# A spectral block and a feed-forward block in one kernel: the first stage in written orders, the first chunk handed over already transposed

## The chip, the cores and the metric

The kernel runs on one core of one Trainium2 chip. Times are device microseconds (us). The measure is the median of separate runs; a profile is one further execution, and it gives a time of its own and a span (first to last instruction).

The engines are called as the profile calls them: PE (TensorE, matmuls), DVE (VectorE), ACT (ScalarE), POOL (GpSimd) and SP (SyncE, which here only issues DMAs, in order).

## The reference

```python
def _layernorm(x, axis=-1, eps=1e-5):
    m = jnp.mean(x, axis=axis, keepdims=True)
    v = jnp.var(x, axis=axis, keepdims=True)
    return (x - m) / jnp.sqrt(v + eps)

# x [1, 2048, 512] bf16, A_w_r and A_w_i [2048, 257], w1 [512, 1792], w2 [1792, 512]
X = rfft2(layernorm(x)) * (A_w_r + 1j * A_w_i)     # over both axes, float32
h = x + irfft2(X, s=(2048, 512)).astype(bf16)
u = einsum("bsd,df->bsf", layernorm(h), w1) + b1
r = maximum(u, 0)
out = h + einsum("bsf,fd->bsd", r * r, w2) + b2
```

## The kernel before

The 2048 rows are held as 16 tiles of 128 rows (`xs[:, g, :]`, g from 0 to 15). The two-dimensional transform is done as chains of matmuls against sine and cosine tables that the kernel makes itself.

**Front.** POOL and DVE make integer index tables, ACT turns them into sines: `KF` (the 128-point mask table, made on DVE at L342 from `kft`), `GF`, `EF` (parts 0 and 1 by sine, part 2 the negative of part 0). DVE takes the row statistics of 14 of the 16 tiles (`st`, L393, then `mv`, L395), ACT those of tiles 3 and 6 (L384, L387). POOL raises the variance to the power -1/2 (`rs`, L400), and each tile's scaled table `KR` is `KF` times `rs`: tiles 0 to 7 on POOL, 8 and 9 on ACT, 10 to 15 on DVE. PE multiplies each tile by its `KR` (L416, L417), and ACT and DVE copy the result into `Bt` (L432 on ACT for tiles 0 to 9, L448 for 10 to 15).

**Middle.** For eight pairs of blocks `pr` = 0 to 7 there follow: matmuls `p2` (L516; the first one needs all of `Bt`), the copy `U` (L526), matmuls `p3` (L495, with `EF`), the copy `AB` (L593; L554 for pair 0), on DVE the sum and difference `X` (L600), the product with the spectral weights `m` (L614), `Z` (L624) and `M` (L635, L637), matmuls `p4` (L654 to L662, with the transposed tables `EI`), and the copy into `T2` (L677). `EI` parts 0 and 1 come from SP's DMA transposes of `EF` (L453), part 2 is made by ACT from part 0 (L482). `EN` (L485, in the order lists `EI-3-6`) is a negated slice of `EI`, used by pair 6 alone. The inverse table `GI` is made by ACT in the middle (L260). Weights arrive in two halves: the natural rows (`Wn`, L283 and L284) and the reversed rows, which are first copied inside DRAM (`wx`, L279) and then loaded (`Wr`, L287). Pair 0 needs only `Wn`; every other pair needs both.

**Hand-over.** For tiles 0 and 1 (chunk 0): matmuls `pd` (L738), copies `EO` (L743), matmuls `py` that add the residual and give h in natural layout (L828 to L833), the statistics of h (tile 0 on ACT, L689; tile 1 on DVE, L843 and L845), a square root (L846), reciprocal (L849), normalization `u` (L857, L859), PE transposes (L868), the copy `UT` (L874), and then the first matmuls of the feed-forward part.

**Feed-forward.** Chunks of 2, 3, 4, 4 and 3 tiles: for each, 14 up-projections (L936), ReLU with bias on ACT (L948), the square on DVE (L954), the down-projections (L965), the residual (L974) and the store. The spectral tail of the later chunks (L765 to L820) is put between the up-projections.

**What sets the order.** `Plan` holds tasks with an engine, a guessed duration, the keys that they read and write and a priority. It picks for each engine the task that can start first by its own guesses; `lag` is how long after its issue a DMA is guessed to land, and `order` only fixes a sequence in the plan. `plan.run(MID)` takes the middle's order of PE, ACT and DVE from lists of names written by hand. The program's order on each engine is then fixed (`pin`); on the chip an instruction waits for what it really depends on. In PSUM, `mm` tiles have three slots in the middle and `sg` tiles two.

```python
dve(1.14, prod, z, reads=[("X", pr), ("Wn", 0), ("Wn", 1), ("Wr", 0), ("Wr", 1)],
    writes=[("m", pr)], alloc=("m", ("m", pr)))
act(0.37, lambda pr=pr: sc.activation(EN[:, BY_Z.index(pr)], EI[:, 0:2, pr], ACT.Identity, scale=-1.0), 84.0,
    reads=[("EI", 0), ("EI", 1)], writes=[("EI", 3, pr)])
"ACT": "U-2 AB-1 U-3 AB-2 U-5 AB-3 EI-2 b1f U-4 AB-5 U-6 AB-4 T2-0 T2-1 U-7 GI EI-3-6 AB-6 T2-2 "
       "AB-7 T2-3 T2-5 sqrt T2-4 T2-6 T2a-0 T2b-0",
```

Of the kernel before, what the change touches and what calls it, by code (L numbers as in the profile page):

```python
# [15 lines left out]
P = 128  # L16
# [17 lines left out]
class Plan:  # L34
# [55 lines left out]
    def run(self, line=None):  # L90
# [8 lines left out]
        while any(left.values()):  # L99
            best = None  # L100
            for e, ts in left.items():
                cand = []
                for t in ts if e not in lines else [t for t in ts if t["name"] == lines[e][0]] if lines[e] else []:
# [29 lines left out]
            if e in lines:  # L133
                lines[e].pop(0)
# [10 lines left out]
def kernel(  # L145
# [47 lines left out]
    mv2 = persist.tile([P, 2], FP32, name="mv2")  # L193
    st2 = persist.tile([P, 6], FP32, name="st2")
# [22 lines left out]
    cE = tab.tile([P, 1], FP32, name="cE")  # L217
    rowq = tab.tile([P, 2, 16], I32, name="rowq")
# [50 lines left out]
    CH = ((0, 2), (2, 4), (4, 6), (6, 8), (8, 12), (12, 16))  # L269
    LAND = (2.65, 3.85, 4.55, 5.2, 5.95, 6.7)  # L270
# [3 lines left out]
    add("SP", 0.2, lambda: sy.dma_start(b1b[:], B_b1.rearrange("(i p) -> i p", p=P)), writes=["b1b"], prio=5.5, at=0.7, lag=8.0)  # L274
# [3 lines left out]
    for i in range(2):  # L278
        add("SP", 2.0, lambda i=i: sy.dma_start(wx[i][:].rearrange("k j l -> j k l"),  # L279
                                                wv[i].rearrange("k j l -> j k l")[9:16, ::-1, 1:L + 1]),  # L280
            writes=[("wx", i)], prio=6 + i, at=1.0, lag=5.0)
    for i in range(2):
        add("SP", 1.0, lambda i=i: (sy.dma_start(W[:, i], wv[i][:, 0:8, 1:L + 1]),  # L283
                                        sy.dma_start(W[:, 2 + i, 0], wv[i][:, 8, 1:L + 1])), writes=[("Wn", i)],  # L284
            prio=8 + i, at=1.0, lag=12.0)
    for i in range(2):
        add("SP", 1.0, lambda i=i: sy.dma_start(W[:, 2 + i, 1:8], wx[i][:, ::-1]), reads=[("wx", i)], writes=[("Wr", i)],  # L287
            prio=10 + i, lag=10.5)
# [29 lines left out]
    pool(0.1, lambda: gp.memset(ident[:], 0.0), 390.0, writes=["id0"], order=[("KR", G - 1)])  # L318
    pool(0.3, lambda: gp.affine_select(out=ident[:], in_=ident[:], compare_op=ALU.not_equal, fill=1.0, base=0,
                                       pattern=[[-1, P]], channel_multiplier=1), 390.0, reads=["id0"], writes=["ident"])  # L320
    pool(0.34, lambda: iota(idxD[:], [[1, 256]], 0, 0), 395.0, writes=["idxD"], order=[("KR", G - 1)])
# [15 lines left out]
    for t in range(2):  # L337
# [4 lines left out]
    dve(0.48, lambda: ve.scalar_tensor_tensor(  # L342
        KF[:].rearrange("p h (q s) -> p (h q) s", s=8), sub8[:].unsqueeze(1).to_broadcast([P, 32, 8]), pF[:, 2:3],
        flat(kft[:]).unsqueeze(2).to_broadcast([P, 32, 8]), ALU.is_equal, ALU.mult),
        0.7, reads=["kft", "pF", "sub8"], writes=["KF"], shared=True)
# [7 lines left out]
    for t in range(2):  # L353
        act(0.62, lambda t=t: sin_of(flat(GF[:, t]), lo(flat(fiG[:, t]))), 0.6 + t / 10, reads=[("fiG", t)],
            writes=[("gf", t)])
    dve(0.15, lambda: ve.tensor_scalar(GF[:, :, :, 255:256], GF[:, :, :, 255:256], 0.5, None, ALU.mult), 54.0, reads=[("gf", 0), ("gf", 1)],
        order=[("KR", G - 1)], writes=["GF"])
    for i in range(2):
        act(1.16, lambda i=i: sin_of(flat(EF[:, i]), lo(fiE[i][:])), 0.5 + i / 10, reads=[f"fiE{i}"],
            writes=[f"EF{i}"])  # L360
    dve(0.46, lambda: ve.tensor_scalar(EF[:, 2], EF[:, 0], -1.0, None, ALU.mult), 78.0, reads=["EF0"],
        order=["BtD"], writes=["EF2"])
# [17 lines left out]
    for bi, (a, b) in enumerate(BATCH):  # L380
# [38 lines left out]
    for g in range(BIG):  # L419
# [10 lines left out]
        def e1(g=g, key=key):  # L430
            dst = Bt[:].rearrange("p e q (g s) -> p e g q s", s=8)[:, :, g - 1:g + 1]
            sc.copy(dst, T[key][:].rearrange("p (i e q s) -> p e i q s", e=4, q=16, s=8))  # L432
        if g % 2:
            act(0.93, e1, 10 + g, reads=[key], writes=["Bt"] + ["Btw"] * (g == BIG - 1))
    for a, b in UNITS:
        n = b - a
        for t in range(2):
            k, eng = ("p1", a, t), ("ACT", "DVE")[t]
# [7 lines left out]
            def e2(a=a, b=b, t=t, k=k, eng=eng):  # L446
                dst = Bt[:, 2 * t:2 * t + 2].rearrange("p e q (g s) -> p e g q s", s=8)[:, :, a:b]
                COPY[eng](dst, T[k][:, 0:256 * (b - a)].rearrange("p (i e q s) -> p e i q s", e=2, q=16, s=8))  # L448
            add(eng, ((0.37, 0.59), (0.42, 0.67))[t][n - 1], e2, reads=[k] + ["Btw"] * t, order=[("va", 4)] * t,
                writes=["Bt"] + ["BtD"] * (t == 1 and b == G), prio=56 + a)  # L450

    def tr_dma(i, dst, src, dep, prio):
        add("SP", 2.5, lambda: sy.dma_start(dst, src, transpose=True), reads=dep, writes=[("EI", i)], prio=prio, lag=(10.6, 10.4, 0, 8.0)[i])  # L453
    for i in range(2):
        tr_dma(i, EI[:, i], flat(EF[:, i]), [f"EF{i}"], 12 + i)
    tr_dma(3, KI[:], flat(KF[:]), ["KF"], 16)
    for k, (d, s) in ((0, (W1[:], B_w1.rearrange("(c p) f -> p c f", p=P))),
# [7 lines left out]
    dve(0.25, lambda: ve.tensor_scalar(CN[:, 0:len(BY_PE)], EF[:, 1, PE0:8], -1.0, None, ALU.mult), 75.0, reads=["EF1"],  # L465
        order=["EF2"], writes=["CN"])
    dve(0.13, lambda: ve.tensor_copy(pF[:, 5:7], pI[:, 5:7]), 0.75, reads=["p2"], writes=["pF2"], shared=True)
    for lt in range(4):
        pool(0.48, lambda lt=lt: gp.tensor_scalar(fiI[:, lt], idxD[:], pF[:, 5 + lt % 2:6 + lt % 2],
                                                  float((QT, HT)[lt // 2]), ALU.mult, ALU.add), 400.0,  # L470
             reads=["pF2", "idxD", ("KR", G - 1)], writes=["fiI"])
    dve(0.15, lambda: ve.tensor_scalar(nm1[:], mv1[:, :, 0], -1.0, None, ALU.mult), 190.0,
        reads=[("mv", g) for g in range(G)], order=["EF2"], writes=["nm0"])
    dve(0.15, lambda: ve.tensor_scalar(nm1[:, 3:7:3], nmr[:, 3:7:3], 1.0 / RT, None, ALU.mult), 190.0,
        reads=["nm0"], writes=["nm1"], shared=True)

    def mid_tasks():
        def b1t():
            mm(sg_tile(("b1",))[:, 0:NF], lhsT=b1b[:], rhs=ident[0:NF, 0:NF], start=True, stop=True)
        add("PE", 0.07, b1t, reads=["b1b", "ident"], order=[("p3", 3)], writes=[("b1",)], prio=141.0, alloc=("sg", ("b1",)))  # L480
        act(0.19, lambda: sc.copy(b1f[:], T[("b1",)][:, 0:NF]), 142.0, reads=[("b1",)], writes=["b1f"])
        act(1.1, lambda: sc.activation(flat(EI[:, 2]), flat(EI[:, 0]), ACT.Identity, scale=-1.0), 83.0, reads=[("EI", 0)],  # L482
            order=["EF2", ("X", 0, 0)], writes=[("EI", 2)])
# [3 lines left out]
        act(1.07, lambda: sin_of(flat(GI[:]), lo(flat(fiI[:]))), 142.0, reads=["fiI"], order=[("p3", 4)], writes=["GI"])  # L487
        act(1.4, lambda: sc.activation(junk[:, 0:1], eps[:], ACT.Sqrt), 0.0, reads=["GI", "eps", ("p4", SQ)], writes=["sqrt"])
# [8 lines left out]
    for pr, first in ((0, 1), (1, 1), *((p, 0) for p in range(8))):  # L497
        z = Z0 + 10 * pr
        if (pr, first) == (0, 0):
            plan.run()  # L500
# [121 lines left out]
        def zz(pr=pr, r=0):  # L622
            Z = buf(fwd, ("Z", pr), "Z", [P, 2, 2, 256], BF16, 2) if r == 0 else T["Z", pr]
            ve.tensor_tensor(Z[:, :, r], T["m", pr][:, :, 0, r], T["m", pr][:, :, 1, 1 - r], (ALU.subtract, ALU.add)[r])  # L624
# [18 lines left out]
        def s4(pr, part, lts):  # L643
            key = ("p4", pr, "t", lts[0] // 2) if pr == 7 else ("p4", pr)
            pt = T[key] if part else (sg_tile if pr == 7 else mm_tile)(key)
            src = T["M" if pr and pr not in BY_Z else "Z", pr][:].rearrange("p u r (j e) -> p u r e j", e=2)
            for lt in lts:
                r, e = lt // 2, lt % 2
                k = lt - lts[0] if pr == 7 else lt
# [11 lines left out]
                else:  # L661
                    mm(o, lhsT=src[:, part, r, e, :], rhs=EI[:, 1 - part:3 - part, pr, :],  # L662
                       start=part == 0 and e == 0, stop=part == 1 and e == 1)
        for h in range(2):
            for k in range(2) if pr == 7 else (None,):
                lts = {None: range(4) if pr else (2 * h, 2 * h + 1), 0: (0, 1), 1: (2, 3)}[k]
                add("PE", 0.92 if pr in BY_Z else 0.46 if k is None else 0.23, lambda pr=pr, h=h, s4=s4, lts=lts: s4(pr, h, lts),
                    reads=[("Z", pr) if pr == 0 else ("ZM"[pr not in BY_Z] + "h" * (1 - h), pr), ("EI", 0), ("EI", 1), ("EI", 2)]
                    + [("EI", 3, pr)] * (pr in BY_Z), order=[("p4", pr, 0, k)] * h, uses=[("ZM"[pr > 0 and pr not in BY_Z], pr)],
                    writes=[("p4", pr, h, k)] + [("p4", pr)] * (k is None) + [("p4", pr, "t", k)] * (k is not None),  # L670
                    name=f"p4-{pr}-{h}" + "ab"[k] * 1 if k is not None else f"p4-{pr}-{h}", prio=z + 32 * (pr < 5),
                    alloc=(("mm", ("p4", pr)) if k is None else ("sg", ("p4", pr, "t", k))) if h == 0 else None)

        def et(eng=sc.copy, pr=pr, a=0, b=G, l0=0, l1=4):
            dst = T2[:, l0:l1, a:b, 2 * pr:2 * pr + 2, :].rearrange("p l g q s -> p l q g s")
            src = T["p4", 7, "t", l0 // 2] if pr == 7 else T["p4", pr]
            eng(dst, src[:].rearrange("p (l q g s) -> p l q g s", q=2, g=G, s=8)[:, :, :, a:b])  # L677
# [332 lines left out]
```

## Time and profile before

| | |
|---|---|
| median of 3 runs | 160.2 us (159.95 to 160.39) |
| time of the profiled execution | 160.21 us |
| its span | 158.4 us, 2890 instructions |
| granted clock of PE | 1.0 throughout |
| PE busy | 152.0 us (96% of the span) |
| DVE, ACT, POOL busy | 119.0, 102.5, 33.1 us |

The span splits into stages at these points of the trace: to 18.6 us the front, to 45.3 us the middle, to 51.7 us the hand-over of chunk 0, to 155.5 us the feed-forward part, where PE is busy 103.7 of 103.8 us, and a last output and store. PE also runs matmuls on a zero tile (L243, L368, L716) where the plan sees a gap, so its busy share before 51.7 us says little; which instruction waits for which is what counts there.

### The profile page before, as it was taken

To read this page: it belongs to the slowest core of one execution; us is meant where nothing else is said; L and a number is where in the kernel's file an instruction comes from. 1 tells how busy PE (TensorE), PEld (TensorE's weight loads), DVE (VectorE), ACT (ScalarE), POOL (GpSimd) and SP (SyncE) were. 2 spreads that over 40 slices of the span, in tenths; PEclk is the share of its full clock that TensorE was granted. 3 is DMA by queue.
4 is the path that set the end of the run, shared out by engine and by line. 5 is a ranking of instruction groups with operands and counts; after the bars stand their busy time and mean duration, and the time that the engine had idled before them with its cause. 6 is when DMAs were issued, how large, how long until landed. Compare 5 with 4: busy or idle time off the path is not lost.

```text
span 158.4 us, 2890 instructions
## 1 busy us (share of the span) xinstructions
PE 152.0 (96%) x1027; PEld 91.9 (58%) x1027; DVE 119.0 (75%) x322; ACT 102.5 (65%) x189; POOL 33.1 (21%) x83
## 2 busy tenths in 40 slices
PE   6998999999798999999999999999999999999992
PEld 4587876787477886565544544444544444565471
DVE  5999988999867987889952989991599962285221
ACT  8989679999967887297801899530588820188000
POOL 8798700000000033022240013440002240000000
DMA  4957999994000001104132000314000312010011
GB/s 128 320 187 219 242 226 218 387 363 140 0 4 0 0 4 35 35 33 35 35 66 67 33 0 4 66 35 132 33 0 0 69 36 66 33 35 4 0 66 33
DMA packets 21017, 13.43 MB, mean 85 GB/s; under 512 B 9738, under 2 KB 19722, under 8 KB 21002
## 3 DMA queue, kind: packets, MB, share of 16 engines
q1 hardware_dynamic: 21002, 13.25, 31.3%
q8 instruction: 8, 0.13, 0.3%
q14 instruction: 7, 0.06, 0.1%
HBM read 8.92 MB, written 3.01 MB: 75 GB/s over the span
## 4 chain that ended last, share of the span: by engine, by line
PE 74%; DVE 15%; DMA 4%; issue 3%; SPq 1%; ACT 1%; POOL 0%; ACTq 0%
PE po L965 31%; PE sg L936 20%; PE ph L936 10%; DMA xs<-in_A_x_dram 4%; DVE Z L624 3%; DVE m L614 3%; DVE st L393 3%; DVE X L600 2%; PE m_p L516 2%; PE pp L788 1%; DVE M L635 1%; PE pp L795 1%; SPq L272 1%; DVE M L637 1%; PE s_p L516 1%
## 5 line engine op out<-in xcount | busy, mean ns | idle before, releaser
L965 PE MATMUL po<-W,act 128*128 128x512 bf16 (+1 forms) x238 | 50.0, 366 | 0.0
L948 ACT ACTIVATE rl<-sg,b1f 128x384 bf16<-128x384 f32 (+2 forms) x46 | 27.3, 601 | 21.9 <-PE sg L936 20.6
L936 PEld LDWEIGHTS <-W 128*128 128x128 bf16 x288 | 26.8, 98 | 19.7 <-issue 0.2
L936 PE MATMUL sg<-UT,W 128*128 128x384 bf16 (+2 forms) x184 | 37.2, 337 | 0.0
L965 PEld LDWEIGHTS <-act 128*128 128x128 bf16 x238 | 23.2, 98 | 24.0
L954 DVE TENSOR_TENSOR act<-rl 128x384 bf16<-128x384 bf16 (+2 forms) x70 | 25.0, 367 | 6.5 <-ACT rl L948 6.0
L974 DVE TENSOR_TENSOR ot<-po,hb 128x512 bf16<-128x512 f32 (+1 forms) x17 | 11.2, 658 | 20.7 <-PE po L965 20.5
L880 POOL TENSOR_SCALAR rs<-ss 128x1 f32<-128x1 f32 x14 | 6.1, 435 | 90.5 <-ACT junk L689 90.5
L948 ACT ACTIVATE rl<-ph,b1f 128x512 bf16<-128x512 f32 (+2 forms) x23 | 13.8, 602 | 10.0 <-PE ph L936 9.4
L936 PE MATMUL ph<-UT,W 128*128 128x512 bf16 (+3 forms) x96 | 19.9, 330 | 0.1
L816 DVE TENSOR_TENSOR hs<-pp,xs 128x512 bf16<-128x512 f32 x14 | 9.6, 689 | 2.3 <-PE pp L788 1.3
L689 ACT ACTIVATE junk<-hs,nm 128x512 bf16<-128x512 bf16 x14 | 10.0, 714 | 0.1
L495 PE MATMUL m_p<-U,EF 128*128 128x512 bf16 (+1 forms) x46 | 9.5, 337 | 0.0
L393 DVE BATCH_NORM_STATS2 st<-xs 128x6 f32<-128x512 bf16 x14 | 9.0, 672 | 0.6 <-DMA xs<-in_A_x_dram 0.6
L811 DVE TENSOR_TENSOR R<-q 128x127 bf16<-128x127 f32 x40 | 9.4, 283 | 0.0
L820 DVE TENSOR_TENSOR hb<-hs,b2b 128x512 f32<-128x512 bf16 x14 | 9.1, 681 | 0.0
L882 POOL TENSOR_TENSOR rs<-rs,mhalf 128x1 f32<-128x1 f32 x14 | 8.0, 569 | 1.2
L778 DVE TENSOR_TENSOR q<-pp,od 128x256 f32<-128x256 f32 x20 | 7.6, 415 | 0.0
L243 PEld LDWEIGHTS <-fz 128*128 128x128 bf16 x59 | 5.0, 113 | 4.2 <-issue 2.3
L516 PE MATMUL m_p<-GF,Bt 128*128 128x256 bf16 x56 | 7.4, 273 | 0.0
L677 ACT CAST T<-m_p 128x1024 bf16<-128x1024 f32 x7 | 7.1, 1057 | 0.5 <-PE m_p L659 0.5
L593 ACT CAST AB<-m_p 128x1024 bf16<-128x1024 f32 x7 | 7.3, 1046 | 0.0
(163 smaller groups left out, 227.6 us busy)
## 6 DMA issues: line engine op xcount, KB each, us to landing
W<-in_B_w_dram SPq DMA_DIRECT2D x2, 1792.0 KB, 10.7
out_dram<-ot SPq DMA_DIRECT2D x15, 128.0 KB, 1.8
xs<-in_A_x_dram SPq DMA_DIRECT2D x4, 256.0 KB, 3.8
xs<-in_A_x_dram SPq DMA_DIRECT2D x2, 512.0 KB, 6.7
W<-wx SPq DMA_DIRECT2D x2, 448.0 KB
W<-in_A_w_r_dram SPq DMA_DIRECT2D x1, 512.0 KB, 8.0
W<-in_A_w_i_dram SPq DMA_DIRECT2D x1, 512.0 KB, 6.4
wx<-in_A_w_r_dram SPq DMA_DIRECT2D x1, 448.0 KB
```

The source lines that it names most:

```text
L393: ve.bn_stats(st[:], xs[:, g, :])
L495: mm(o.rearrange("p (j i e) -> p j i e", e=2, i=RUN), lhsT=w, rhs=U[:, q, s].rearrange("p (j e i) -> p j i e", e=2, i=RUN), **k)
L516: mm(puv[:, e, :], lhsT=Bt[:, 2 * t + 1 - e, 2 * pr + q, :], rhs=gfv[:, t, :, e, :], start=(t == 0), stop=(t == 1))
L689: sc.activation(junk[:], src, ACT.Square, bias=nm1[:, g:g + 1], accum_out=ss2[:, g:g + 1])
L811: ve.tensor_tensor(o, x, y, (ALU.add, ALU.subtract, ALU.subtract, ALU.add)[k])
L816: dve(0.66, lambda g=g: ve.tensor_tensor(hs[:, g, :], T["p6", g][:], xs[:, g, :], ALU.add), z, reads=[("p6", g)], writes=[("hs", g)])
L820: add(("DVE", "POOL")[HBP], (0.62, 1.3)[HBP], lambda g=g: (ve, gp)[HBP].tensor_tensor(hb[:, g, :], hs[:, g, :], b2b[:], ALU.add), prio=lat ...
L936: mm(p[:, P * i0:P * i1], lhsT=W1[:, d, bass.ts(f, P)], rhs=T["UT", c][:, i0:i1, d, :], start=(d == 0), stop=(d == ND - 1))
L948: sc.activation(r[:, 0:P * n], T["ph", c, f][:, 0:P * n], ACT.Relu, bias=b1f[:, f:f + 1], scale=1.0)
L954: ve.tensor_tensor(t[:, f, 0:P * n], r[:, 0:P * n], r[:, 0:P * n], ALU.mult)
L965: mm(p[:, cs], lhsT=T["act", c][:, f, bass.ts(i, P)], rhs=W2[:, f, cs], start=(f == 0), stop=(f == NF - 1))
L974: ve.tensor_tensor(o[:, cs], T["po", g, h][:, cs], hb[:, g, cs], ALU.add)
```

## The change

It touches the front, the middle and the hand-over; the feed-forward part stays but for the PSUM tag of one early up-projection and some order keys.

- The front gets written orders for all five engines, SP included (`FRONT`), the middle gets new ones (`MID`), and the hand-over gets some (`DRAIN`).
- `KF` is made by POOL with a two-input multiply. `KR`, the `Bt` copies, `GF`'s correction, `EF` part 2, `CN` and `nm1` may now sit on other engines; by the lists DVE makes `KR` of tiles 5, 7, 10, 13 and 15, ACT of 12, POOL the rest; DVE copies `Bt-9` and `Bt-12-1`, ACT all other `Bt`; POOL makes `EF` part 2.
- `GI` moves into the front on ACT, in two halves. `EI` part 2 becomes a third DMA transpose.
- The fifth load of x (4 tiles) becomes two of 2. SP's order becomes x, `b1b`, `Wn`, `wx`, `EI-0`, `Wr`, `EI-1`, `EI-2`, `EI-3` (`KI`), feed-forward weights.
- In the middle, `p3-1` goes ahead of `p2-2`, `EI-3-6` to the third place on ACT, and `Z` of pair 6 gets a layout in which its two halves don't interleave.
- Chunk 0 is made transposed: `yt` collects mean correction (`cen`), residual (`res`) and spectral part with the feature dimension on the partitions; ACT squares it, PE sums over partitions with a matrix of ones, ACT takes the root, DVE the reciprocal, and one DVE multiply gives `UT`. The natural-layout `py` stays, for the residual of the output.

```diff
-    CH = ((0, 2), (2, 4), (4, 6), (6, 8), (8, 12), (12, 16))
+    CH = ((0, 2), (2, 4), (4, 6), (6, 8), (8, 10), (10, 12), (12, 16))
...
-            prio=8 + i, at=1.0, lag=12.0)
+            prio=6.4 + i / 20, at=1.0, lag=9.0)
...
-        add("SP", 1.0, lambda i=i: sy.dma_start(W[:, 2 + i, 1:8], wx[i][:, ::-1]), reads=[("wx", i)], writes=[("Wr", i)],
-            prio=10 + i, lag=10.5)
+        add("SP", 1.0, lambda i=i: sy.dma_start(W[:, 2 + i, 1:8], wx[i][:, ::-1]), reads=[("wx", i)], order=[("EI", 0)], writes=[("Wr", i)],
+            prio=10 + i, lag=8.0)
...
-    dve(0.48, lambda: ve.scalar_tensor_tensor(
-        KF[:].rearrange("p h (q s) -> p (h q) s", s=8), sub8[:].unsqueeze(1).to_broadcast([P, 32, 8]), pF[:, 2:3],
-        flat(kft[:]).unsqueeze(2).to_broadcast([P, 32, 8]), ALU.is_equal, ALU.mult),
-        0.7, reads=["kft", "pF", "sub8"], writes=["KF"], shared=True)
+    pool(0.5, lambda: gp.tensor_tensor(
+        KF[:].rearrange("p h (q s) -> p (h q) s", s=8), sel[:].unsqueeze(1).to_broadcast([P, 32, 8]),
+        flat(kft[:]).unsqueeze(2).to_broadcast([P, 32, 8]), ALU.mult), 0.95, reads=["kft", "sel"], writes=["KF"])
...
+    tr_dma(2, EI[:, 2], flat(EF[:, 2]), ["EF2"], 15)
...
-        act(1.1, lambda: sc.activation(flat(EI[:, 2]), flat(EI[:, 0]), ACT.Identity, scale=-1.0), 83.0, reads=[("EI", 0)],
-            order=["EF2", ("X", 0, 0)], writes=[("EI", 2)])
...
+            FRONT = {
+                "PE": "fa-0 fa-1 fa-2 fa-4 fa-6 fa-5 fa-3 p1a-0 p1-0 p1a-1 p1-1 p1a-2 p1-2 p1a-3 p1-3 p1a-4 "
+                     "p1a-10-1 p1-10-1 p1a-10-0 p1-10-0 p1a-12-0 p1-4 p1-15-0 p1-15-1 p1a-12-1 p1-12-0 p1-12-1 "
+                     "p1-14-0 p1-14-1 p2-1-0 p2-0-0 p2-0-1 p2-1-1 p3-0-0 p3-0-1",
+                "ACT": "sinset kft gf-0 fiE0 sm-3 GI mv-3 GI0 sm-6 EF0 mv-6 gf-1 Bt-1 Bt-3 Bt-5 Bt-7 KR-12 "
+                      "Bt-10-1 Bt-10-0 Bt-15-0 Bt-15-1 Bt-12-0 Bt-14-0 Bt-14-1 EF1 U-0-0 AB-0-0 AB-0-1",
+                "DVE": "eps fz mv1z p02 p01 pF pF2 fiG-0 fiK sel fiG-0+1 cE st-0 st-1 st-2 mv-0 mv-1 mv-2 va-0 "
+                      "st-4 st-5 mv-4 st-7 mv-5 mv-7 va-1 st-8 st-9 mv-8 mv-9 KR-5 st-11 va-2 mv-11 st-10 st-12 "
+                      "mv-10 mv-12 KR-7 va-3 st-15 st-14 mv-15 KR-10 va-5 st-13 mv-14 mv-13 va-4 nm0 qtc GF "
+                      "KR-15 KR-13 Bt-9 Bt-12-1 U-1-0 U-0-1 U-1-1",
+                "POOL": "p0 p7 p1 sub8 idxG p2 offq0 rowq0 idxD offq rowq idxE fiI+1 fiI+3 mhalf fiG-1 fiI+2 "
+                       "fiG-1+1 fiI KF rs-0 KR-1 KR-0 rs-1 KR-2 KR-3 KR-4 rs-2 KR-6 KR-8 rs-3 KR-11 KR-9 rs-5 "
+                       "rs-4 KFq KR-14 nm1 fiE1 id0 EF2 ident CN",
+                "SP": "x-1 x-3 x-5 x-7 x-9 x-11 x-15 b1b Wn-0 Wn-1 wx-0 wx-1 EI-0 Wr-0 Wr-1 EI-1 EI-2 EI-3 FW-0 "
+                     "FW-1 FW-3",
...
     MID = {
...
+        "PE": "p3-1 p2-2-0 p2-2-1 p2-3-0 p2-3-1 p2-5-0 p3-2 p2-5-1 p3-3 b1 p2-4-0 p2-4-1 p3-5 p3-4 "
+             "p2-6-0 p2-6-1 p4-0-0 p4-0-1 p2-7-0 p2-7-1 p4-2-0 p4-2-1 p3-6 p4-1-0 p4-1-1 p3-7 p4-3-0 "
+             "p4-3-1 p4-5-0 p4-5-1 p4-6-0 p4-6-1 yt-1-0 yt-1-1 p4-4-0 p4-4-1 yt-0-0 p4-7-0a p4-7-0b "
+             "p4-7-1a p4-7-1b yt-0-1 pd-0-1 pd-0-0 pd-1-1 pd-1-0",
+        "ACT": "AB-1 U-2 EI-3-6 U-3 AB-2 U-5 AB-3 b1f U-4 nmt AB-5 AB-4 U-6 T2-0 U-7 T2-2 sqrt AB-6 T2-1 "
+              "AB-7 T2-3 T2-5 T2-6 T2-4 T2a-1 EO-0-0 EO-1-0",
...
-            ve.tensor_tensor(Z[:, :, r], T["m", pr][:, :, 0, r], T["m", pr][:, :, 1, 1 - r], (ALU.subtract, ALU.add)[r])
+            ve.tensor_tensor(Z[:, r] if pr in BY_Z else Z[:, :, r], T["m", pr][:, :, 0, r], T["m", pr][:, :, 1, 1 - r],
+                             (ALU.subtract, ALU.add)[r])
...
+    def cen(g):
+        mm(sg_tile(("yt", g))[:], lhsT=ones[0:2, :], rhs=nmt[:, g].unsqueeze(1).to_broadcast([2, ND, P]), start=True, stop=False)
+
+    def res(g):
+        for d in range(ND):
+            mm(T["yt", g][:, P * d:P * d + P], lhsT=xs[:, g, P * d:P * d + P], rhs=ident[:], start=False, stop=False)
...
+                def yt6(g=g, k=0):
+                    o = T["yt", g][:].rearrange("p (a d c) -> p d a c", a=2, c=P)
+                    for d in range(2):
+                        mm(o[:, d], lhsT=EO[:, g, k, P * d:P * d + P],
+                           rhs=KI[:] if k else KI[:, 0].unsqueeze(1).to_broadcast([P, 2, P]), start=False, stop=k == 1 and d == 1)
+
+                act(0.6, lambda g=g: sc.activation(flat(sq0[:, g]), T["yt", g][:], ACT.Square), -30.0, reads=[("yt", g, 3)],
+                    writes=[("sq", g)], uses=[("yt", g)])
+
+                def ssm(g=g):
+                    p = bank(("ss", g), "pp" if g else "ph", 3 if g else 1)
+                    for d in range(ND):
+                        mm(p[:, 0:P], lhsT=ones[:], rhs=sq0[:, g, d], start=d == 0, stop=d == ND - 1)
...
+                act(0.3, lambda g=g: sc.activation(rsb[:, g], T["ss", g][:, 0:P], ACT.Sqrt, bias=eps[:], scale=1.0 / D), -30.0,
+                    reads=[("ss", g), "sqrt"], writes=[("sd", 0, g)])
+                dve(0.27, lambda g=g: ve.reciprocal(rsb[:, g], rsb[:, g]), -30.0, reads=[("sd", 0, g)], writes=[("r2", 0, g)])
+
+                def ut0(g=g):
+                    u = buf(ffn, ("UT", 0), "UT", [P, 4, ND, P], BF16, 2) if g == 0 else T["UT", 0]
+                    ve.tensor_tensor(u[:, g], T["yt", g][:].rearrange("p (d c) -> p d c", c=P),
+                                     rsb[:, g].unsqueeze(1).to_broadcast([P, ND, P]), ALU.mult)
...
+    DRAIN = {
+        "PE": "yt-0-2 yt-0-3 yt-1-2 yt-1-3 py-1-0 ss-0 py-1-1 py-0-0 ss-1 p5-3 p5-2 py-1-2 py-0-1 p5-4 "
+             "pf-1 py-0-2 pf-0 ph-0-0 ph-0-7",
```

## The prediction

> **What bounds the kernel now.** I read the chain that ended last, by engine, then the busy time by stage (columns: stretch, its length, then PE, PEld, DVE, ACT and POOL busy with counts, PE's clock, DMA share, GB/s).
>
> ```profile
> PE 74%; DVE 15%; DMA 4%; issue 3%; SPq 1%; ACT 1%; POOL 0%; ACTq 0%
> ```
> ```profile
> 9.00:18.60 9.60, 9.11 (x93) 7.67 (x89) 9.33 (x31) 8.15 (x13) 8.71 (x17) 1.00 0.77 219
> 18.60:45.30 26.70, 25.63 (x207) 18.76 (x205) 24.34 (x52) 24.56 (x31) 0.51 (x2) 1.00 0.77 204
> 45.30:51.70 6.40, 5.85 (x73) 4.71 (x71) 4.77 (x14) 4.58 (x13) 0.00 (x0) 1.00 0.01 3
> 51.70:155.50 103.80, 103.69 (x618) 56.04 (x615) 73.05 (x200) 56.97 (x120) 16.91 (x42) 1.00 0.15 36
> ```
>
> The last stage is PE alone and is not changed, so the question is only how much earlier PE reaches its steady stream (51.7 us). In the front DVE leads (97% busy), in the middle PE and DVE are both nearly full. The PE timeline of the middle shows no gap from 18.6 to 40.2 us; then:
>
> ```profile
> 40.60 1.28 PE L662 MATMUL m_p<-EI,M 128*128 128x256 bf16 x8 [0.41 <-ACT T L677]
> 43.27 0.28 PE L659 MATMUL m_p<-EN,Z 128*128 128x256 bf16 x1 [0.52 <-DVE Z L624]
> 44.40 1.05 PE L662 MATMUL s_p<-EI,M 128*128 128x256 bf16 x8
> ```
>
> From 40.19 us to 45.28 us, when the last `p4` has issued, is 5.09 us. The matmuls in it are 8 + 16 + 8 of 0.11 us, 3.5 us: about 1.5 us are waits for DVE, and for the copy on ACT. The hand-over, from the chain in order of time (start, length, what):
>
> ```profile
> 46.00 0.65 PE pp L738 x6
> 48.22 0.71 DVE st L843
> 49.16 0.29 ACT rs L846
> 49.46 0.73 ACT u L859
> 50.24 0.41 PE po L868 x4
> 50.67 0.43 DVE UT L874
> 51.15 0.38 PE ph L936 x4
> ```
>
> Tile 1's up-projections start at 51.71 us (PE timeline), 6.43 us after 45.28. SP's timeline (start, length) gives the fourth thing to watch, the tables and weights on one DMA queue:
>
> ```profile
> 5.02 4.75 SPq L279 DMA_DIRECT2D wx<-in_A_w_i_dram  x1
> 16.10 3.30 SPq L453 DMA_TRANSPOSE EI<-EF  x1
> 19.50 1.22 SPq L287 DMA_DIRECT2D W<-wx  x2
> 20.77 2.59 SPq L453 DMA_TRANSPOSE EI<-EF  x1
> ```
>
> **What the Trainium skill says.** "GPSIMD Engine Reference", section Engine selection: POOL takes about twice VectorE's time for two-input elementwise work and runs one-input work at roughly line rate. The trace does not bear out the second, a `KR` of 128x256 (one input) takes 0.28 us on DVE and 0.48 on POOL; no two-input tile of that size runs on POOL here, so the first is untested. "DMA: Bandwidth & Descriptors", section Two DMAs through the same engine are not ordered: a DMA that reads what another wrote must wait for its completion semaphore; here `Wr` after `wx`. "ScalarE: Activation LUTs", section What ACT_TABLE_LOAD costs: an ACTIVATE is 186 ns plus 0.833 ns an element, and 93 more for a pointer operand; L689, with pointer and 512 elements, should be 706 ns and is 687.
>
> **The front, part by part.** DVE loses `KF` (0.47) and one of six late `KR`; its 14 `st` (0.585 from start to start) and `mv` (0.11) stay. The fifth load in two can save the 0.19 us that DVE waited at 8.96. `KF` on POOL costs 0.47 us (as on DVE) to 0.94 (twice it); I take 0.6. Before it POOL has all index work, so it comes at 6.6 to 7.2 instead of 4.5. Queued behind it are `rs-0` and `KR-0`, which PE waits for: 7.2 + 0.65 + 2 x 0.45 = 8.75, against the first L416 at 8.95. From there I walk POOL: `rs` of four 0.98, of three 0.85, of two 0.73, of one 0.57, `KR` 0.45. `rs-4` ends at 16.15 us (before: about 16.4), `KR-14` at 16.75. DVE's `va-4` ends at about 15.3, so DVE stands waiting for `rs-4`, then `KR-13` to 16.6, `Bt-9` 1.2 and `Bt-12-1` 0.6: 18.45. ACT, now with `GI` (2 x 0.52) and less `Bt`, is full from 3 us and ends `Bt-14-1` at 18.5. So `p2` starts at 18.5, against 18.59: **no gain in the front**, give or take 0.5.
> Then `EF1`, late because `fiE1` is last but two on POOL (to 18.1), keeps ACT until 19.6, `U-0-0` until 20.15; `EF2` on POOL (1152 elements as `fiE`, 1.2 us) ends at 19.4, ahead of its use at 20.3. `p3-1` waits for `U-1-1` on DVE to 21.5. `p3-1` and `p2-2` are done at 23.25 against 23.12: 0.1 us late for PE. DVE's `m-1` can begin at 24.2 instead of 25.25, since `p3-1` goes first.
>
> **The middle.** ACT loses `EI` part 2 (1.22) and `GI` (1.11), off the path. DVE, 1 us ahead, and pair 6's separate halves remove what PE waited for after 40.19: up to 1.46 us. PE gains two 128-column matmuls for the mean (0.11) and of `cen` and `res` (each 0.22, twice) three of four before `p4-7` ends, 0.66. Balance for the end of `p4`: +0.1 - 1.46 + 0.77 = -0.6, so 44.7 us.
> Against it stands one added wait. `EI-3-6` is now third on ACT, at 24.35, and reads `EI` part 1. Queued behind it are `U-3`, `AB-2` and so `p3-3` on PE and `X-2` on DVE. Part 1 landed at 20.77 + 5.9 = 26.7 before. Now its source is ready at 19.6 only, and SP first waits for `wx-1`, which moves behind `Wn`. DMA ran `wx` at 152 GB/s (9.5 to 14 us) and `Wn` at 300 (14 to 18.5); in the new order `Wn` is through at 13.2 and `wx` at 18, landing at 19.3. `Wr-1` issues then, to 19.9 instead of 20.7, its data lie before the transpose. A transpose alone: KI (2 blocks) took 3.0, `UT` (4 blocks) 2.4, and 9 blocks issue for 2.6, so some 4 us: 23.7 with a free queue, 26.7 if nothing changes. ACT is late from 24.4 on, and PE by the same amount: 0 to 2.3 us. I take 0.3. `Wr-1` itself should land near 24; DVE's `m-1` can be 1.2 us late before PE feels it. `EI-2` and `KI` are put off by 2.6 us of issue, to 29 or so; `p4-0` needs them at 30.5. The feed-forward weights issue 2.5 us later and landed 10 us before use: nothing. So `p4` ends at 45.0, **0.3 us earlier**.
>
> **The hand-over**, from the last `p4` (E): `T2a-1` at 0.2 on ACT, 0.3 long; `pd` at 0.65, 1.1; `EO` 0.37 each with hops of 0.2, the last done at 1.9; the four `yt` matmul groups (0.22) end at 2.5. ACT: `sq-0` 2.15 to 2.75, `sq-1` to 3.3 (186 + 427 = 613 ns by the page, L743's 0.37 for 256 elements in line); ones-matmuls 0.22 and latency 0.2; roots at 3.35 and 3.9 (0.25 each); DVE: reciprocal 0.2, multiply 0.6 (L974's kind, 0.66), twice: 3.65 to 4.5, 4.5 to 5.3. Tile 1's up-projection at 5.4 against 6.43; tile 0's run at 4.6. Gone are `st`, `mv`, `nr`, `u`, the transposes and their copy. `py` and `p5` are in PE's idle time from 2.5 to 4.6 (6 x 0.22 + 3 x 0.25). **1.0 us earlier**; bounds 0.5 (multiply and root at their longest, DVE's `T2b` in the way) and 1.6.
>
> **Sum:** 0.3 + 1.0 = 1.3 less; I give 0.1 back for small hops. The profiled execution has 160.21 us (158.4 span and 1.8 around it), the median 160.2, so 159.0. A difference within 0.3% (0.5 us) can't be told from none.
>
> **Rivals.**
> *Half of it.* The stalls of the middle come back elsewhere, since PE and DVE are both nearly full (for: 25.6 and 24.3 of 26.7 us), and the hand-over gives 0.6: 159.7.
> *The early `EI-3-6` makes it slower.* Part 1 lands as late as before or later: for it speak 26.7 before, `Wr` ahead of it in the queue, and a source that is ready 11 us later than before; against it the shorter way to `Wr-1`. At 26.7 ACT stands for 2.3 us, PE and DVE get it in full: 159.0 - 0.3 + 2.3 = 161.0. It decides from a landing of about 26 on, where the stall eats the gain.
> *The front does gain.* DVE's own sum from 3.88 (14 `st` and `mv`, five `KR`, `Bt`) is 13.6, to 17.5 us; were its waits for POOL small and ACT 0.6 quicker, `p2` starts at 17.7 and all moves: 158.0.
> *Nothing happens* needs a hand-over gain that just pays for 1 us of ACT waiting: 160.2.
>
> **How the numbers follow.** Forecast 0.5; half 0.2; slower 0.15; front 0.15. Low 157.6 takes in the front with a hand-over at its better bound, high 161.0 the late transpose. The forecast's own range is 158.3 to 159.6. Faster by over 0.3% are forecast, front and a third of half, 0.71; within, 0.16; slower 0.13.
>
> **What would show it.** `p2` (L516) near 18.5; no waits of PE after 40 us; ACT's `EN` (L485) starting at 24.4 with little idle before it; last `p4` near 45.0; first up-projections (L936) at 49.6, tile 1's at 50.4. Wrong, if ACT stands before `EN` for over 1 us, if PE waits for `EF` or `U` before 24 us, or if DVE waits for a DMA at `m-1`.

## The result and the profile after

The changed kernel takes **162.40 us** (median, lowest 162.34), the kernel before 160.19 in the same comparison: a ratio of 1.0142, 95% interval 1.0121 to 1.0163. One of its four runs (164.9 us; with it the median is 162.51) was in a slower state of the chip, as were four of the eighteen of e2 below, and these five are left out of the medians and ratios here. It is slower, where 159.0 was forecast. The profiled execution has 162.63 us and a span of 160.9 us, against 160.21 and 158.4, so the trace has 2.4 to 2.5 us to explain.

The page's line of the chain that ended last, by engine, of the changed kernel:

```profile
PE 77%; DMA 8%; SPq 6%; DVE 4%; ACT 2%; issue 1%; DVEq 0%
```

DVE's share of the chain has fallen from 15% to 4%, and DMA and SP's queue have come into it: a transfer now has a part in what decides before the steady stream. The chain names `wx` (6%) and `Wr` (2%) and goes on through DVE's `m-1` to an ACT copy `U`. The reading below finds another transfer, the transpose of `EI`; e7 decides between the two. Busy time by stage of the changed kernel, cut at its own points (columns: stretch, length, then PE, PEld, DVE, ACT, POOL busy with counts, PE's clock, DMA share, GB/s):

```profile
9.00:18.40 9.40, 8.57 (x87) 7.31 (x84) 8.56 (x29) 8.55 (x16) 8.95 (x16) 1.00 0.85 232
18.40:46.50 28.10, 26.30 (x213) 19.39 (x212) 24.31 (x49) 23.75 (x30) 2.86 (x8) 1.00 0.78 205
46.50:54.10 7.60, 5.88 (x59) 4.02 (x58) 5.38 (x10) 3.32 (x9) 0.00 (x0) 1.00 0.01 2
54.10:157.80 103.70, 103.60 (x616) 55.95 (x615) 72.37 (x198) 59.22 (x123) 17.08 (x42) 1.00 0.15 36
```

The feed-forward part is as long as before (103.7 us against 103.8). The front is 0.2 us shorter. The middle has grown from 26.7 to 28.1 us, and 1.8 us of it PE is idle (1.1 before). The hand-over has grown from 6.4 to 7.6 us. These two are all but 0.1 us of the loss: the last `p4` (E in what follows, read at the start of the matmul behind it) has issued at 46.52 us instead of 45.28, 1.24 later, and tile 1's up-projections start 7.56 us after it instead of 6.43, 1.13 more; together 2.37.

**The middle.** PE's timeline of the changed kernel has one stall between 22 us and the end of `p4`, and none of the three that stood behind 40 us before:

```profile
27.60 1.02 PE L510 MATMUL m_p<-U,EF 128*128 128x512 bf16 x4 [1.73 <-ACT U L557]
```

PE waits 1.73 us for a `U` that ACT copies late. ACT's timeline says why (start, length, what, in brackets the idle time ahead of it and what ended it):

```profile
23.33 1.02 ACT L557 CAST U<-m_p 128x1024 bf16<-128x1024 f32 x1
26.23 0.42 ACT L496 ACTIVATE EN<-EI 128x256 bf16<-128x256 bf16 x1 [1.88 <-DMA EI<-EF]
26.55 1.00 ACT L557 CAST U<-m_p 128x1024 bf16<-128x1024 f32 x1
```

`EN` (`EI-3-6` in the list) stands third on ACT and waits 1.88 us for the transpose of `EI` part 1; the `U` copy that PE needs is queued behind it. SP's timeline shows that transpose in second place of an x2 line, issued from 20.75 us:

```profile
11.37 2.44 SPq L286 DMA_DIRECT2D wx<-in_A_w_i_dram  x1
13.93 4.87 SPq L458 DMA_TRANSPOSE EI<-EF  x1
18.90 1.76 SPq L294 DMA_DIRECT2D W<-wx  x2
20.75 4.43 SPq L458 DMA_TRANSPOSE EI<-EF  x2
```

The x2 line is parts 1 and 2; part 1 leads it, behind `Wr` (L294), and lands at 26.2 us, 5.5 us after its issue.

DVE waited for a transfer here too:

```profile
25.26 1.22 DVE L645 TENSOR_TENSOR m<-X,W 128x2048 bf16<-128x2048 bf16 x1 [0.76 <-DVE X L631]
```

This is `m-1`. The profile puts its wait down to `X`, which had been done for 0.76 us. `Wr-1`, which `m-1` also reads, was issued at 20.29 and landed 4.9 us later by the trace, at 25.2, just before `m-1` starts.

**The hand-over.** From the chain in order of time (start, length, what):

```profile
47.23 0.62 DVE T L711
47.85 0.34 DVE EO L733
48.24 0.39 PE s_yt L872 x2
48.64 0.41 PE s_yt L872 x2
49.07 1.09 ACT sq L879 x2
50.16 0.36 ACT rsb L887
50.54 0.96 DVE rsb L889
51.68 0.69 DVE UT L893
52.37 0.87 DVE rsb L889
53.34 0.70 DVE UT L893
54.08 0.38 PE ph L973 x4
```

The four DVE steps at the end, reciprocal, multiply, reciprocal, multiply, run one behind the other from 50.54 to 54.04 us, and PE waits for each multiply (0.55 and 0.83 us by its timeline). A reciprocal (L889) takes longer than the multiply on four times as many elements.

### The profile page after: what moved, and what is told of

The parts are those of the page before. It is cut to its first block, busy times and chain, and to the rows that moved or that the text cites. A ratio compares the mean times of both kernels' runs of the same rounds, so it can differ in the third digit from the quotient of the medians.

```text
span 160.9 us, 2881 instructions
## 1 busy us (share of the span) xinstructions
PE 151.2 (94%) x1017; PEld 91.1 (57%) x1017; DVE 118.5 (74%) x311; ACT 101.8 (63%) x190; POOL 37.2 (23%) x92
## 4 chain that ended last, share of the span: by engine, by line
PE 77%; DMA 8%; SPq 6%; DVE 4%; ACT 2%; issue 1%; DVEq 0%
PE po L1002 30%; PE sg L973 20%; PE ph L973 10%; DMA wx<-in_A_w_i_dram 6%; PE m_p L510 4%; PE m_p L694 3%; SPq L291 3%; DMA W<-wx 2%; SPq L279 2%; PE m_p L547 2%; PE pp L832 1%; DVE rsb L889 1%; PE pp L839 1%; PE m_p L691 1%; DVE UT L893 1%
## 5 line engine op out<-in xcount | busy, mean ns | idle before, releaser
L985 ACT ACTIVATE rl<-sg,b1f 128x512 bf16<-128x512 f32 (+2 forms) x46 | 27.4, 603 | 19.3 <-PE sg L973 17.9
L973 PE MATMUL sg<-UT,W 128*128 128x512 bf16 (+3 forms) x188 | 37.4, 334 | 0.6 <-DVE UT L893 0.6
L973 PE MATMUL ph<-UT,W 128*128 128x384 bf16 (+3 forms) x100 | 20.5, 328 | 0.8 <-DVE UT L893 0.8
L985 ACT ACTIVATE rl<-ph,b1f 128x384 bf16<-128x384 f32 (+2 forms) x24 | 14.3, 596 | 10.8 <-PE ph L973 10.2
L510 PE MATMUL m_p<-U,EF 128*128 128x512 bf16 (+1 forms) x46 | 9.5, 337 | 1.7 <-ACT U L557 1.7
L929 ACT ACTIVATE u<-hs,nr,rs 128x512 bf16<-128x512 bf16 x6 | 4.9, 816 | 6.7 <-POOL nr L921 6.7
L510 PEld LDWEIGHTS <-EF 128*128 128x128 bf16 x52 | 5.1, 97 | 4.6 <-issue 1.9
```

What stands on the lines that cost most here:

```text
L510: mm(o.rearrange("p (j i e) -> p j i e", e=2, i=RUN), lhsT=w, rhs=U[:, q, s].rearrange("p (j e i) -> p j i e", e=2, i=RUN), **k)
L973: mm(p[:, P * i0:P * i1], lhsT=W1[:, d, bass.ts(f, P)], rhs=T["UT", c][:, i0:i1, d, :], start=(d == 0), stop=(d == ND - 1))
L985: sc.activation(r[:, 0:P * n], T["ph", c, f][:, 0:P * n], ACT.Relu, bias=b1f[:, f:f + 1], scale=1.0)
```

## The experiments

My theory after the result: two losses that add, the wait of `EN` for the transpose and the two reciprocals. Two rivals stood against it: the natural layout was simply the better hand-over, whatever the reciprocal costs, or the waits only move when one of them is taken away. All runs are set beside the kernel before, which had medians of 160.23 (first four), 160.43 (next four) and 160.35 us (last two) in its comparisons. E and tile 1 come from one profile of each kernel, and e3 and e10, one kernel, differ in E by 0.25 us. Tile 1 is the start of its first up-projection; for some runs it is the second half of an x8 row and worked out from that row's start.

| kernel | median, us | ratio to before (95%) | E | tile 1 | from E |
|---|---|---|---|---|---|
| before | 160.2 | | 45.28 | 51.71 | 6.43 |
| changed | 162.40 | 1.0142 (1.0121 to 1.0163) | 46.52 | 54.08 | 7.56 |
| e1, `EN` late | 161.24 | 1.0070 (1.0046 to 1.0095) | 44.88 | 52.44 | 7.56 |
| e2, copy for reciprocal | 161.19 | 1.0053 (1.0036 to 1.0069) | 46.80 | 52.9 | 6.1 |
| e3, `EN` late, one root | 159.74 | 0.9962 (0.9944 to 0.9980) | 44.76 | 50.60 | 5.84 |
| e4, natural | 161.32 | 1.0057 (1.0033 to 1.0081) | 46.19 | 52.75 | 6.56 |
| e5, natural, `EN` late | 160.06 | 0.9984 (0.9970 to 0.9997) | 44.80 | 51.36 | 6.56 |
| e6, `wx` first | 162.43 | 1.0115 (1.0080 to 1.0151) | 46.38 | 53.94 | 7.56 |
| e7, part 1 ahead of `Wr` | 163.34 | 1.0178 (1.0141 to 1.0214) | 47.09 | 54.65 | 7.56 |
| e8, e3 and `EO` apart | 159.15 | 0.9927 (0.9902 to 0.9952) | 44.72 | 50.57 | 5.85 |
| e9, e3 and `EO` by tile | 159.10 | 0.9925 (0.9907 to 0.9944) | 44.70 | 50.48 | 5.78 |
| e10, e3 again | 159.31 | 0.9944 (0.9925 to 0.9962) | 45.01 | 50.86 | 5.85 |

**e1: the wait alone.** `EI-3-6` moves behind `U-7` in ACT's written order; nothing else.

```diff
-        "ACT": "AB-1 U-2 EI-3-6 U-3 AB-2 U-5 AB-3 b1f U-4 nmt AB-5 AB-4 U-6 T2-0 U-7 T2-2 sqrt AB-6 T2-1 "
+        "ACT": "AB-1 U-2 U-3 AB-2 U-5 AB-3 b1f U-4 nmt AB-5 AB-4 U-6 T2-0 U-7 EI-3-6 T2-2 sqrt AB-6 T2-1 "
```

> The changed kernel with one name moved: EI-3-6 (EN, L496) stands behind U-7 in ACT's order instead of third. Theory (ACT's 1.9 us wait for the transposed EI part 1 went to PE in full): p3-3 starts at 25.9 instead of 27.6, no wait of ACT before EN, the last p4 about 1.7 us earlier, time 162.5 - 1.7 = 160.8. Rival (the reversed W half is late too: m-1 began at 25.26 after a wait of 0.8 us, and DVE is the next bound): half of it comes back as waits of PE for Z and M after 35 us, time about 161.6.

E comes at 44.88, 1.64 us earlier than in the changed kernel. The profiled execution is 1.65 us lower (160.98), the median 1.16. PE's timeline of e1, at the place of the stall:

```profile
25.38 0.60 PE L547 MATMUL m_p<-GF,Bt 128*128 128x256 bf16 x4
25.81 1.03 PE L510 MATMUL m_p<-U,EF 128*128 128x512 bf16 x4
```

The `p3-3` matmuls (L510) that started at 27.60 run at 25.81 with no wait ahead of them. No other wait takes its place before E. The hand-over is 7.56 us as before, so the remaining 1.0 us to the kernel before isn't in the middle. One thing e1 leaves open: in its profile the transfers ran about 0.6 us earlier, and `m-1` starts at 24.64 with no wait, so here both waits are gone. e7 separates them.

**e2: the reciprocal alone.** The division is left out: DVE copies the root instead.

```diff
-                dve(0.27, lambda g=g: ve.reciprocal(rsb[:, g], rsb[:, g]), -30.0, reads=[("sd", 0, g)], writes=[("r2", 0, g)])
+                dve(0.27, lambda g=g: ve.tensor_copy(rsb[:, g], rsb[:, g]), -30.0, reads=[("sd", 0, g)], writes=[("r2", 0, g)])
```

> The changed kernel with the two reciprocals of the hand-over (L889, 128x128) replaced by plain DVE copies of the same tiles, so the division is left out. Theory (the reciprocal was sized at 0.2 us and takes 0.95, twice in series on DVE): the copies take about 0.2, tile 1's first up-projection comes 1.5 us earlier, time 161.0. Rival (the hand-over is long by its hops, the roots and the multiplies, and the second tile waits for ACT anyway): at most 0.7 us earlier, time 161.8 or more.

DVE's groups, shapes kept apart (busy time, mean ns of one, idle ahead), first of the changed kernel, then of e2:

```profile
L889 DVE RECIPROCAL rsb<-rsb 128x128 f32<-128x128 f32 x2 | 1.9, 948 | 1.4 <-ACT rsb L887 1.4
```
```profile
L889 DVE COPY rsb<-rsb 128x128 f32<-128x128 f32 x2 | 0.4, 222 | 1.4 <-ACT rsb L887 1.4
```

On the same tile the reciprocal takes 948 ns and a copy 222. Twice in series that is 1.45 us, and the hand-over is about 1.45 us shorter (6.1 against 7.56). The median gains 1.21, less than theory's 1.5. In this profile E was 0.28 us later than in the changed kernel, with `EN`'s wait still there (2.06 us). The rival's mark, 161.8 or more, was not reached.

**e3: both, with the division kept.** `EN` late, and ACT's root becomes its inverse root, so the reciprocals go altogether. ACT's first use of the function (`sqrt` in its list) is changed with it, and DVE's list loses the two reciprocals; these lines and `EN`'s move are left out here.

```diff
...
-                act(0.3, lambda g=g: sc.activation(rsb[:, g], T["ss", g][:, 0:P], ACT.Sqrt, bias=eps[:], scale=1.0 / D), -30.0,
-                    reads=[("ss", g), "sqrt"], writes=[("sd", 0, g)])
-                dve(0.27, lambda g=g: ve.reciprocal(rsb[:, g], rsb[:, g]), -30.0, reads=[("sd", 0, g)], writes=[("r2", 0, g)])
+                act(0.3, lambda g=g: sc.activation(rsb[:, g], T["ss", g][:, 0:P], ACT.Abs_reciprocal_sqrt, bias=eps[:], scale=1.0 / D), -30.0,
+                    reads=[("ss", g), "sqrt"], writes=[("sd", 0, g), ("r2", 0, g)], name=f"sd-0-{g}")
...
```

> EI-3-6 behind U-7 as in e1, and Sqrt on ACT plus reciprocal on DVE replaced by one ACT instruction (Abs_reciprocal_sqrt) for each tile. Theory (both costs are separate and add): 1.7 for the wait, 1.5 to 1.9 for the reciprocals and a hop, time 159.0, below the kernel before. Rival (one hides behind the other, or DVE bounds the middle): 160 or more.

159.74 us, 2.66 less than the changed kernel and 0.4% faster than the kernel before. The two gains add: 1.16 (e1) and 1.21 (e2) make 2.37, and here the DVE copy of e2 is gone too (from E to tile 1 it is 5.84 us, not 6.1). ACT's and DVE's timeline of e3:

```profile
48.37 0.37 ACT L887 ACTIVATE rsb<-ph,eps 128x128 f32<-128x128 f32 x1
48.83 1.29 DVE L892 TENSOR_TENSOR UT<-s_yt,rsb 128x512 bf16<-128x512 f32 x2 [1.48 <-issue]
```

The inverse root takes 0.37 us, just what the root took, and the two multiplies follow one another. "ScalarE: Activation LUTs", section What it computes, advises VectorE's reciprocal with a square-root ACTIVATE in place of `Rsqrt`, for accuracy. These are the two steps of the changed kernel, there with the root first, and here they cost two DVE steps of 0.95 us on the path; `Abs_reciprocal_sqrt` is not among the functions of which that section warns.

**e4 and e5: chunk 0 natural again**, from `py` through `st`, `mv`, `rs`, `nr`, `u` and the transposes to `UT` as in the kernel before, with the new orders of front and middle kept, less the entries for `yt` and its mean; the written order of the hand-over goes with the layout. e4 with `EN` third on ACT, e5 with it late.

```diff
-    def cen(g):
...
-    def res(g):
...
-                def yt6(g=g, k=0):
...
+                def d6(g=g, k=0):
...
-    UPT = ("ph", "sg")
+    UPT = ("ph", "po")
-    plan.run(DRAIN)
+    plan.run()
```

> The changed kernel with chunk 0 made in natural layout again, as before the change (py, statistics, normalization, PE transposes, copy); front and middle orders stay, without the yt matmuls and their mean. Theory (the transposed chain was 1.1 us longer than the one it replaced, and its matmuls lay in a middle that PE fills): last p4 to tile 1's first up-projection 6.4 us instead of 7.6, and up to 0.6 us of PE less in the middle, time 160.9 to 161.4. Rival (the transposed chain is no longer than the natural one, and all of the loss comes from the front and the middle): 162.5 or more.

> Chunk 0 natural again and EI-3-6 behind U-7; the written orders of front and middle stay. Theory (the two losses are separate, 1.3 us of ACT waiting and about 1 us of hand-over): 161.3 - 1.3 = 160.0 us (159.7 to 160.4), level with the kernel before; last p4 near 44.7, tile 1's up-projection 6.5 us after it. Rival (the transposed hand-over costs nothing, its loss only shows while ACT is late): 161.2, as the transposed one with EI-3-6 late.

With the wait in place the natural layout takes 161.32 us and E is still at 46.19: of the middle's 1.24 us the layout of chunk 0 accounts for some 0.33, little more than E differs between two profiles of one kernel. Without the wait it takes 160.06, theory's number. Its hand-over is 6.56 us in both, the kernel before's 6.43 and little more. So the rival of e5 is out, and the layouts can be compared cleanly with `EN` late: natural 6.56, transposed with root and reciprocal 7.56, transposed with one inverse root 5.84. **The transposed layout with one inverse root is 0.7 us better than the natural one, and the reciprocals turn that into 1.0 us worse.** In the ratios to before, e3 and e10 are 0.2 and 0.4% below e5. The natural layout kept its own root and its reciprocals of one element (148 ns each, L849 of the kernel before). What one inverse root would save there was not tried, so the 0.7 us is not the layout's alone. The orders of front and middle are worth what is left of 45.28 to 44.80, 0.5 us of E; in the median, 0.16% with an interval that reaches from 0.03 to 0.30%, too little to build on.

**e6 and e7: why part 1 lands late.** Both change SP's order alone; e7 also changes the plan's order keys to fit, which are left out here.

```diff
-                "SP": "x-1 x-3 x-5 x-7 x-9 x-11 x-15 b1b Wn-0 Wn-1 wx-0 wx-1 EI-0 Wr-0 Wr-1 EI-1 EI-2 EI-3 FW-0 "
+                "SP": "x-1 x-3 x-5 x-7 x-9 x-11 x-15 b1b wx-0 wx-1 Wn-0 Wn-1 EI-0 Wr-0 Wr-1 EI-1 EI-2 EI-3 FW-0 "
```

That is e6, and this is e7:

```diff
...
-                "SP": "x-1 x-3 x-5 x-7 x-9 x-11 x-15 b1b Wn-0 Wn-1 wx-0 wx-1 EI-0 Wr-0 Wr-1 EI-1 EI-2 EI-3 FW-0 "
+                "SP": "x-1 x-3 x-5 x-7 x-9 x-11 x-15 b1b Wn-0 Wn-1 wx-0 wx-1 EI-0 EI-1 Wr-0 Wr-1 EI-2 EI-3 FW-0 "
```

> Only SP's order: wx-0 wx-1 ahead of Wn-0 Wn-1, as in the kernel before; EI-3-6 stays third on ACT. Theory (Wr waits on SP for wx-1 until 20.23 and holds EI part 1 back by 0.5 us): Wr gone by 20.1, part 1 issued at 20.2 instead of 20.75, ACT's idle before EN 1.4 instead of 1.9, 162.0 us. Rival (the order of wx and Wn is the whole cause of the wait): EN at 24.4 without idle, 161.2. Second rival (the landing depends on what is queued, not on the issue): idle unchanged at 1.9, 162.5.

> Only SP's order: the transpose EI part 1 ahead of Wr-0 and Wr-1. Theory (part 1 comes late because Wr's data lie ahead of it): issued at 19.9, when EF1 is there, landed by 24.3, EN without a wait; Wr issues at 22.5 to 23.8 and m-1 on DVE waits for it until 26 or so, 0.7 later than now, of which PE feels 0 to 0.7: 161.2 to 161.9 us. Rival (a transpose takes 5 to 6 us with or without Wr ahead): landed at 25.4, EN idle 1 us and m-1 late on top: 162.5 or more.

In e6 SP issues part 1 at 19.98, 0.77 us earlier (SP's timeline of e6):

```profile
18.65 1.28 SPq L294 DMA_DIRECT2D W<-wx  x2
19.98 5.00 SPq L458 DMA_TRANSPOSE EI<-EF  x2
```

but ACT's timeline has `EN` only 0.15 us earlier, and the time is the same:

```profile
26.08 0.42 ACT L496 ACTIVATE EN<-EI 128x256 bf16<-128x256 bf16 x1 [1.77 <-DMA EI<-EF]
```

So neither the place of `wx` nor 0.77 us in the moment of issue sets the landing; the second rival was right, and my theory of e6 fell. e7 shows what does. With part 1 ahead of `Wr`, the ACT and DVE timelines read:

```profile
24.19 0.42 ACT L496 ACTIVATE EN<-EI 128x256 bf16<-128x256 bf16 x1
27.14 1.23 DVE L645 TENSOR_TENSOR m<-X,W 128x2048 bf16<-128x2048 bf16 x1 [2.69 <-DMA W<-wx]
```

`EN` runs with no wait, so part 1 had landed by 24.2 us, at most 4.3 us after its source (`EF` part 1, ready at 19.91 in e7). It is `Wr`'s data ahead of it that cost the other 2 us. e7 also settles which wait held PE in the changed kernel. The ACT copy behind `EN`, and the `p3-3` matmuls that read it, now run on time, although `m-1` is later than ever:

```profile
24.51 1.00 ACT L557 CAST U<-m_p 128x1024 bf16<-128x1024 f32 x1
25.65 1.03 PE L510 MATMUL m_p<-U,EF 128*128 128x512 bf16 x4
```

So the stall came from `EN`. The link from `m-1` to `U` in the chain of the changed kernel is not one that `U` depends on: here `U` runs 2.6 us before `m-1`. But `Wr`'s data are now late themselves: `m-1` starts 1.88 us later than in the changed kernel, where I had expected 0.7. The time, 163.34 us, lies outside the 161.2 to 161.9 that I expected and is no better than the changed kernel's (the intervals of the two ratios overlap). That price is an upper one: with `m-1` late by the plan's estimate too, it put 45 zero matmuls (L250) into PE's list between 32 and 43 us, and how much of PE's delay they cover or cause was not separated. Two transfers want the queue between 20 and 26 us, and one of them must wait. e1's answer, to need part 1 later, shows no such price.

**e8, e9, e10: the rest of the hand-over.** In the kernels so far ACT's first `EO` copy starts just as DVE's first one ends, later than its matmuls. e8 and e9 start from e3. e8 puts `EO` in four tiles; e9 leaves `EO` alone and gives both halves of tile 0 to DVE and both of tile 1 to ACT; e10 is e3 once more.

```diff
-    EO = persist.tile([P, 2, 2, 256], BF16, name="EO")
+    EO = [[persist.tile([P, 256], BF16, name=f"EO{g}{e}") for e in range(2)] for g in range(2)]
...
```

That is e8, and this is e9, in ACT's and DVE's lists:

```diff
-              "AB-7 T2-3 T2-5 T2-6 T2-4 T2a-1 EO-0-0 EO-1-0",
+              "AB-7 T2-3 T2-5 T2-6 T2-4 T2a-1 EO-1-1 EO-1-0",
...
-              "T2a-0 T2b-1 EO-0-1 EO-1-1 T2b-0",
+              "T2a-0 T2b-1 EO-0-1 EO-0-0 T2b-0",
```

> As the kernel with EI-3-6 late and one root on ACT (159.74 us), and EO in four tiles instead of one. Theory (ACT's EO-0-0 waits 1.02 us only because DVE writes another part of the same tile): ACT's first EO starts 0.4 us earlier, yt of tile 0 and all behind it too: first up-projection near 49.5, 159.3 us. Rival (the wait is for the matmuls of pd or comes from their bank, not from the EO tile): unchanged, 159.7.

> As the kernel with EI-3-6 late and one root; VectorE copies both halves of EO of tile 0, ScalarE both of tile 1 (before: each engine one half of each tile). Theory (ACT's first EO waits for DVE because both read one PSUM tile, pd of tile 0): ACT's first EO now starts when pd of tile 1 is there, 0.1 to 0.2 us earlier, without a wait for DVE; tile 0's halves are done at the same time as before (2 x 0.41 on DVE), so the first up-projection is where it was, and the time 159.2 to 159.7 us. Rival (the wait comes from something else, such as the writes of EO): ACT's first EO again starts at the end of a DVE copy.

> The kernel with EI-3-6 late and one root once more, beside e9 on one chip. If the time of the one with EO in four tiles (159.15 us) was its own gain, this gives 159.7 again; if the two are one kernel in time, as their traces within 0.05 us say, anything from 159.1 to 159.8.

ACT's timeline of e8, then of e9:

```profile
46.41 0.78 ACT L733 CAST EO<-m_pd 128x256 bf16<-128x256 f32 x2 [1.02 <-DVE EO L733]
```
```profile
46.34 0.65 ACT L733 CAST EO<-m_pd 128x256 bf16<-128x256 f32 x2 [0.97 <-PE m_pd L728]
```

Four `EO` tiles change nothing: the write of `EO` is not what ACT waits for. With each engine on its own `pd` tile the wait for DVE is gone and ACT waits for the matmuls of its tile instead. That points to the shared reading of one PSUM tile; whether the chip or the program's own ordering makes one wait for the other is not shown. It is worth 0.06 us from E to tile 1, within the differences of profiles. e3, e8, e9 and e10 lie at 159.74, 159.15, 159.10 and 159.31 us, and e3 and e10 are one kernel; what e8 and e9 gain over it, if anything, is not shown. All four beat both kernels, by 0.4 to 0.75% over the kernel before.

## Why the prediction was wrong

- **The front was right.** `p2` starts at 18.37 us (forecast 18.5, before 18.59), `KF` on POOL takes 0.62 us (taken 0.6, of 0.47 to 0.94), `EF1` ends at 19.97 (19.6). The rival in which the front gains is refuted by the same line.
- **The stalls of the middle were right.** None is left after 40 us. With the wait removed E is at 44.88 (e1), 44.76 (e3) and 44.80 (e5); the balance without a wait had said 44.7.
- **The added wait of `EI-3-6` was mis-sized.** This is the first step that failed: "I take 0.3", of bounds 0 to 2.3; it is 1.88. The mechanism, its queue on ACT and its victims were named. What failed is the landing of part 1. "Its data lie before the transpose" was written, and then the transpose was priced as one alone (some 4 us, from the smaller `KI` and `UT`). e7 shows that price to be fair without `Wr` ahead (4.3 us at most), and e6 that an earlier issue doesn't help behind it. Behind `Wr`, which itself landed at 25.2 us where 24 was forecast, it took 5.5. The 5.9 of the trace before was misread as well: it belongs to part 0, issued at 16.10 behind the loads of `Wn`, and the trace has no landing of part 1, so the 26.7 of the prediction had no row behind it. Still, it was a row of the same size with loads ahead of it, and I preferred smaller ones. The issue came 0.85 us later than reckoned as well (20.75, not 19.9), because `wx-1` landed at 20.23 and not at 19.3; by e6 that made little difference.
- **The reciprocal was mis-sized.** This is the second step that failed, "reciprocal 0.2": it is 0.95, twice in series. The 0.2 had no row of its own shape behind it; the trace before only has reciprocals of one element. Neither bound of the hand-over (0.5 and 1.6 gained) held this case, where 1.13 is lost. The other terms: the first reciprocal starts 4.02 us after E instead of 3.65 (the root takes 0.37, not 0.25, and the `EO` copies end at 2.5, not 1.9), and from there to the up-projection it is 3.54 us instead of 1.75. Of these the chain gives 1.83 to the two reciprocals, instead of 0.4, and 1.71 to the multiplies and hops, instead of 1.35. In sum 0.37 + 1.43 + 0.36, the 2.16 us between 5.4 and 7.56.
- **The sum closes.** 159.0 with 1.58 more for the wait and 2.16 for the hand-over is 162.74, against 162.63 measured. The rival "The early `EI-3-6` makes it slower" had the right mechanism for the middle, and at 1.9 us of its 2.3, though its 26.7 was the misread row; its 161.0 lacks the hand-over. "Half of it" and "Nothing happens" had no part in it.
- **The marks were right.** ACT idle before `EN` for over 1 us was named as what would make it wrong. So was a DVE wait for a DMA at `m-1`, and that came too, 0.76 us for `Wr-1`: `m-1` starts at 25.26, where 24.2 was forecast, within the 1.2 us of delay that the prediction allowed it. That this cost PE anything is not shown. PE's waits for `EF` or `U` before 24 us were not seen.

## What to carry to other kernels

Price a transfer by a row of its own size with transfers ahead of it, not by scaling smaller ones: here 5.9 us stood in the trace for such a row, 4 us was used, and 5.5 was measured. And look up to which issue a landing belongs, since a median over two issues can be the landing of one. A chain names a likely path and not a proven one: here it led through `m-1`, and only a kernel in which the two waits came apart (e7) told which of them PE felt. Before an operation moves from one column to a whole row, look for its price per element, since a row of one element shows only the fixed part; if there is none, its bound above must be a multiple, and a range that leaves it out is too narrow. When a consumer waits for a transfer in a full queue, moving the consumer (e1) can cost nothing where moving the transfer (e7) hands the wait to the next.

## What the hardware showed

DVE's reciprocal of float32 takes 148 ns for one element a partition (before, L849) and 948 ns for 128 (L889), so (948 - 148) / 127 = 6.3 ns an element; a copy of the same 128 elements takes 222 ns in all. "VectorE: DVE Perf Modes", section First, the fixed hardware budget, says that `Reciprocal` is an iterative divide with a repeat count of 8, which could have been a warning. It gives no time for it; these rows agree in so far as it is much slower than a copy, and how the engine divides no run here shows. ACT's inverse root on the same tile takes 0.37 us, as its root does.
